# An FFN whose opening is ordered by the kernel's list scheduler, with paced loads, one more ordinary f-tile, and w2's two parts kept in DRAM

## The chip, the core and the metric

The kernel runs on one core of one Trainium2 chip. The metric is the device time of one execution in microseconds. TensorE is called PE, VectorE DVE, ScalarE ACT, GpSimd POOL and SyncE SP, as in the profile. PE multiplies, DVE, ACT and POOL work elementwise, and SP issues nearly all DMA transfers, in the order of its own instruction stream.

## The reference

One sequence of 2048 tokens with 640 channels goes through two layers, each with an adaptive layer norm in front and a gate behind. The first layer is a long convolution whose kernel is made from 128 complex exponentials per channel; the second is a gated FFN with 1728 hidden channels.

```python
mod = (_silu(c) @ w_mod).reshape(c.shape[0], 6, 1, -1)
sa, ca, ga, sb, cb, gb = (mod[:, 0], mod[:, 1], mod[:, 2], mod[:, 3], mod[:, 4], mod[:, 5])
h = _layernorm(x, axis=-1) * (1 + ca) + sa
x = x + ga * _A_ref(h, ...)          # rfft, product with the kernel's rfft, irfft, skip
h = _layernorm(x, axis=-1) * (1 + cb) + sb
gate, up = einsum("bsd,df->bsf", h, w1), einsum("bsd,df->bsf", h, w3)
x = x + gb * einsum("bsf,fd->bsd", _silu(gate) * up, w2)
```

Everything is in float32, and the FFN's products keep nearly that precision: each operand is split into a high part (rounded to the form that PE multiplies at full rate, `F32R`) and the remainder, and three products are summed: high by high, high by remainder, remainder by high (`three`, L839).

## The kernel before

**Two ways of ordering.** The first part of the kernel, the convolution, is a graph of tasks. `Plan.add` (L178) gives each task an engine, a duration, the tasks that it waits for, a rank and the buffers that it takes and gives back. `Plan.place` (L187) is a list scheduler: it always starts the task that can start first, and among those that can start within 0.1 us of each other the one of lowest rank. The ranks of most tasks are the long table `RANKS`; a task that is added with `own=True` keeps the rank in its `add`. `Plan.run` (L269) then issues all tasks in this order, and `InOrder` (L147) makes each engine keep it strictly. The second part, the FFN, is written as a program in `ffn` (L1002); there PE keeps the program's order, and the compiler places the instructions of the other engines.

**The convolution's end.** The channels go through the convolution in five blocks of 128. Its spectra end as `zd` in DRAM: each block stores eight pieces of 256 KB (`zt`, L1520 to L1530). The tokens' rows come back from them by one more product, the inverse: `iz` tiles are loaded from `zd`, multiplied by `wd` and added to the input `x2`. The FFN works on four token blocks of 512 tokens, so `x2[b]`, b = 0 to 3, each with four rows of 128 tokens by 640 channels. For blocks 0 and 1 the inverse of the first 512 channels (`cut`) is done before the FFN, in four units of two rows, u = 0 to 3 (`load_z` and `first_rows`, L1221 to L1230). The last 128 channels come from the fifth channel block, so their loads (`izb`, `last_rows`, L674) and products (`last_inverse`, L684) stand at the head of `ffn`. The task `change` (L1200) frees the memory of the kernel generation and issues the loads of `x2[0]` and `wd`; the tasks `fw` and `fs` load and split the weights of the f-tiles 0 and 13.

**The FFN.** The 1728 hidden channels are 13 f-tiles of 128 and a half one, number 13, with 64 gate and 64 up channels in one tile of 128. The token blocks go in two pairs, p = 0 with blocks 0 and 1, p = 1 with blocks 2 and 3. There are two ways to compute a tile's gate and up for both blocks of a pair. `plain` (L937) does one block with 30 matmuls of 128x512 (15 for tile 13). `group` (L883) does both blocks with 54 instead of 60: it multiplies sums and differences of weight halves (`factors`, L819) and of token blocks (`x_sums`, L750, which makes `T1` to `T4`), seven block products in place of eight. In pair 0 the tiles 0 and 13 are plain and 1 to 12 are groups; in pair 1 tile 13 is plain and 0 to 12 are groups.

The hidden tile times `w2` is `down` (L975): 15 matmuls (10 for tile 13) into five accumulators `acc`, one for each 128 output channels. The accumulators are five PSUM banks, so one block at a time: the even block's `down` runs inside the next group (`mid`, L1051), while the odd block's hidden tiles are kept in SBUF. After a pair's groups `late` (L1072) finishes the even block, writes it to the output (`output`, L985: gate on ACT, four PE transposes, an add on DVE; then `store`) and does all 14 `down` of the odd block, in the order 13, 0, 1 to 12. During the first `late` the blocks 2 and 3 are normalized, transposed (`turn_x`, L725) and split for pair 1. The second `late` ends the kernel. The inverse rows 8 to 15, for blocks 2 and 3, run inside the groups 1 to 8 of pair 0 (`inverse_row(7 + m)`, L1055).

**w2.** Each use of a tile of `w2` loads 320 KB (`down_load`, L782) and splits it (`down_split`, L793): the high part on ACT, the remainder on DVE or POOL. That is done for each of the four blocks. The high part, the remainder and the raw tile have two buffers each.

**The opening in order** (L1002 to L1034): the last inverse for blocks 0 and 1; block 0's norm, transposes and splits; `plain(0)` for tiles 0 and 13; the same preparation of block 1; `down` of tile 0; `plain(1)` for tile 0; `down` of tile 13; `plain(1)` for tile 13; the sums `T`; then group 1. POOL does every second remainder of the x splits, two of the four subtractions for `T`, and the weight sums.

Of the kernel before, what the change touches and what calls it, by code (L numbers as in the profile page):

```python
# [10 lines left out]
F32 = mybir.dt.float32  # L11
# [7 lines left out]
P = 128  # L19
L = 2048  # L20
D = 640
# [9 lines left out]
WA = 2  # L31
# [249 lines left out]
class K:  # L281
# [18 lines left out]
    def setup(self):  # L300
# [11 lines left out]
        self.zd = d.tile([32, 2, 64, D], F32, name="zd")  # L312
        self.xv = self.x.rearrange("(t1 q j) d -> q t1 j d", t1=32, q=4, j=NJ)
# [319 lines left out]
    def inverse_load(self, name, pool, tag, bufs, j0, nj, d0, d1, other=None):  # L633

        zv = self.zd.rearrange("f r t d -> (f r) t d")
        z = [pool.tile([P, nj, d1 - d0], F32, name=f"{name}{pr}", tag=f"{tag}{pr}", bufs=bufs) for pr in range(2)]
        for pr in range(2):
            for g in range(2):
                t0 = 16 * (2 * pr + g) + j0
                (other if g and other else self.nc.sync).dma_start(z[pr][g * 64:(g + 1) * 64], zv[:, t0:t0 + nj, d0:d1])  # L640
        return z

    def inverse(self, j0, nj, z, ps, tag, bufs, d0, d1):
        nc = self.nc
        w = d1 - d0
        for j in range(nj):
            for o, n in ((0, w),) if w <= 512 else ((0, 320), (320, 320)):
                py = ps.tile([P, 512], F32, name=f"iy{j0 + j}_{d0 + o}", tag=tag, bufs=bufs)
                for pr in range(2):
                    nc.tensor.matmul(py[pr * 64:(pr + 1) * 64, :n], self.wd[(j0 + j) // 4][:, (j0 + j) % 4, pr, :], z[pr][:, j, o:o + n],  # L650
                                     start=True, stop=True, tile_position=(0, pr * 64))
                x2 = self.x2[(j0 + j) // 4][:, (j0 + j) % 4, d0 + o:d0 + o + n]
                nc.vector.tensor_add(x2, py[:, :n], x2)

    def inverse_unit(self, u, pool, ps, tag, bufs):
        z = self.inverse_load(f"iz{u}", pool, "iz", 2, 2 * u, 2, 0, D)
        self.inverse(2 * u, 2, z, ps, tag, bufs, 0, D)


# [13 lines left out]

    def last_rows(self, b, cut):  # L674

        z = [self.row(f"izb{b}{pr}")[:, :512].rearrange("p (j d) -> p j d", j=4) for pr in range(2)]
        zv = self.zd.rearrange("f r t d -> (f r) t d")
        for pr in range(2):
            for g in range(2):
                t0 = 16 * (2 * pr + g) + 4 * b  # L680
                (self.nc.scalar if g else self.nc.sync).dma_start(z[pr][g * 64:(g + 1) * 64], zv[:, t0:t0 + 4, cut:])
        return z

    def last_inverse(self, b, z, cut):  # L684

        py = self.bank(f"iyb{b}").rearrange("p (j d) -> p j d", j=4)
        for j in range(4):
            for pr in range(2):
                self.pe.matmul(py[pr * 64:(pr + 1) * 64, j], self.wd[b][:, j, pr, :], z[pr][:, j], start=True, stop=True, tile_position=(0, pr * 64))
        x2 = self.x2[b][:, :, cut:]  # L690
        self.nc.vector.tensor_add(x2, py, x2)
# [22 lines left out]
    def ln_norm(self, b, rstd, nb):  # L714
        xn = []
        for j in range(4):
            x = self.row(f"xn{b}{j}")
            if j % 2:
                self.nc.vector.tensor_scalar(x, self.x2[b][:, j, :], rstd[:, j:j + 1], nb[:, j:j + 1], op0=ALU.mult, op1=ALU.add)
            else:  # L720
                self.nc.scalar.activation(x, self.x2[b][:, j, :], AF.Identity, scale=rstd[:, j:j + 1], bias=nb[:, j:j + 1])
            xn.append(x)
        return xn

    def turn_x(self, b, k, xn, X, v, where, pool):  # L725

# [1074 lines left out]
```

## Time and profile before

| | us |
|---|---|
| median of 3 runs | 1042.61 |
| lowest and highest | 1042.16, 1042.9 |
| the profiled execution | 1043.67 |
| its span in the profile | 1041.9 |
| PE busy | 883.4 (85%) |
| DVE busy | 734.5 (70%) |
| ACT busy | 576.8 (55%) |
| POOL busy | 410.2 (39%) |

The span runs from the first to the last instruction of the profile, and all positions below are counted from its start. A busy PE is not PE at its peak: matmuls are pipelined, one overlaps the next, and PE's clock is granted by a throttle (PEclk, 1.00 is full speed). So the start-to-start distance of a row of matmuls is the price of one, not its duration. "Idle before" is the time in which the engine did nothing just ahead of an instruction, and its releaser is the event that came last. In the chain of waits the last instruction is followed back, at each step to what released it; "issue" is time in which the engine waited for nothing that the profile shows. `SPq` and `ACTq` rows are the issuing of DMA transfers, and the time from issue to landing is that of the data.

### The profile page before, as it was taken

To read this page: it belongs to the slowest core of one execution; us is meant where nothing else is said; L and a number is where in the kernel's file an instruction comes from. 1 tells how busy PE (TensorE), PEld (TensorE's weight loads), DVE (VectorE), ACT (ScalarE), POOL (GpSimd) and SP (SyncE) were. 2 spreads that over 40 slices of the span, in tenths; PEclk is the share of its full clock that TensorE was granted. 3 is DMA by queue.
4 is the path that set the end of the run, shared out by engine and by line. 5 is a ranking of instruction groups with operands and counts; after the bars stand their busy time and mean duration, and the time that the engine had idled before them with its cause. 6 is when DMAs were issued, how large, how long until landed. Compare 5 with 4: busy or idle time off the path is not lost.

```text
span 1041.9 us, 20733 instructions
## 1 busy us (share of the span) xinstructions
PE 883.4 (85%) x7979; PEld 693.5 (67%) x7979; DVE 734.5 (70%) x1400; ACT 576.8 (55%) x1070; POOL 410.2 (39%) x423
## 2 busy tenths in 40 slices
PE   1474887798999873879999999997889999999897
PEld 1142756677788741756777788775668888888685
DVE  7998999999999375777767675566365656655422
ACT  6867888889788330543444454554254444444432
POOL 1798798888996010231111111134221121120141
PEclk9987999999999897888999999999999999999998
DMA  9965355423223889212333222341222212220332
GB/s 216 259 211 158 95 129 139 102 72 84 63 63 82 197 218 239 64 51 62 92 90 99 64 57 57 89 114 51 75 64 65 75 51 64 69 58 13 84 94 76
DMA packets 108540, 104.38 MB, mean 100 GB/s; under 512 B 10393, under 2 KB 90521, under 8 KB 107161
## 3 DMA queue, kind: packets, MB, share of 16 engines
q1 hardware_dynamic: 107352, 102.53, 36.6%
q8 instruction: 63, 1.03, 0.4%
q10 hardware_dynamic: 1088, 0.52, 0.2%
q14 instruction: 37, 0.30, 0.1%
HBM read 82.06 MB, written 20.97 MB: 99 GB/s over the span
## 4 chain that ended last, share of the span: by engine, by line
PE 64%; DVE 18%; DMA 8%; issue 4%; ACT 4%; SPq 1%; POOL 0%; POOLq 0%; DVEq 0%; ACTq 0%
PE c L156 18%; PE acc L156 17%; PE X L156 12%; PE ps L156 4%; DVE yy L156 3%; PE kps L156 2%; PE fk L156 2%; PE fz L156 2%; PE fh L156 2%; DVE xx L156 2%; DVE hn L156 2%; DVE fp L156 2%; DMA sp<-in_w_mod 2%; DMA xs<-in_x 2%; PE iy L156 1%
## 5 line engine op out<-in xcount | busy, mean ns | idle before, releaser
L156 PE MATMUL acc<-ah,w2l 128*128 128x512 f32 x280 | 115.4, 412 | 10.7 <-DVE w2l L662 6.4
L156 PE MATMUL acc<-ah,w2h 128*128 128x512 f32 x280 | 116.4, 416 | 9.1 <-ACT ah L661 4.4
L827 POOL TENSOR_TENSOR s<-wr 128x256 f32<-128x256 f32 x25 | 19.0, 762 | 225.2 <-DVE wl L662 96.5
L156 PE MATMUL acc<-al,w2h 128*128 128x512 f32 x260 | 105.2, 405 | 2.9 <-DVE al L662 2.9
L156 POOL TENSOR_TENSOR yy<-e,e 128x512 f32<-128x512 f32 x80 | 86.2, 1094 | 16.1 <-PE kps L156 11.2
L661 ACT ACTIVATE w2h<-w2r 128x640 fp32r<-128x640 f32 x51 | 37.5, 734 | 97.0 <-PE acc L156 81.4
L662 DVE TENSOR_TENSOR w2l<-w2r,w2h 128x640 fp32r<-128x640 f32 x37 | 34.6, 934 | 77.9 <-ACT w2h L661 77.9
L156 POOL TENSOR_TENSOR ph<-p,p 128x1024 int32<-128x1024 int32 x40 | 79.0, 1976 | 6.1 <-ACT tr L156 5.3
L156 PE MATMUL kps<-yy,xx 128*32 128x64 f32 x2560 | 51.3, 234 | 30.9 <-DVE xx L156 20.7
L661 ACT ACTIVATE wh<-wr 128x256 fp32r<-128x256 f32 x100 | 41.7, 418 | 62.6 <-PE X L156 46.9
L156 DVE TENSOR_TENSOR yy<-yy,tr 128x512 f32<-128x512 f32 (+1 forms) x80 | 75.4, 945 | 0.9 <-ACT tr L156 0.6
L156 PEld LDWEIGHTS acc<-ah,w2l 128*128 128x128 f32 x280 | 55.5, 198 | 25.7 <-DVE w2l L662 7.7
L156 PEld LDWEIGHTS kps<-yy,xx 128*32 128x32 f32 x2560 | 44.8, 116 | 40.8 <-issue 24.9
L156 PEld LDWEIGHTS acc<-ah,w2h 128*128 128x128 f32 x280 | 55.4, 198 | 24.1 <-ACT ah L661 5.5
L889 ACT ACTIVATE t<-g 128x512 f32<-128x512 f32 x50 | 31.6, 632 | 60.9 <-DVE g L853 60.9
L661 ACT ACTIVATE wh<-s 128x256 fp32r<-128x256 f32 x100 | 41.0, 410 | 43.2 <-PE c L156 20.6
L156 PEld LDWEIGHTS acc<-al,w2h 128*128 128x128 f32 x260 | 50.8, 195 | 15.3 <-DVE al L662 4.1
L662 DVE TENSOR_TENSOR wl<-s,wh 128x256 fp32r<-128x256 f32 x100 | 42.8, 429 | 23.1 <-ACT wh L661 21.0
L828 POOL TENSOR_TENSOR s<-s,wr 128x256 f32<-128x256 f32 x25 | 19.1, 763 | 98.0 <-issue 84.3
L858 DVE SCALAR_TENSOR_TENSOR g<-t,g 128x512 f32<-128x512 f32 x50 | 34.6, 693 | 32.4 <-ACT t L889 32.1
L662 DVE TENSOR_TENSOR wl<-wr,wh 128x256 fp32r<-128x256 f32 x100 | 43.8, 439 | 19.2 <-ACT wh L661 19.2
L156 ACT ACTIVATE tr<-ph,hpi 128x512 f32<-128x512 f32 x80 | 54.7, 691 | 3.6 <-DVE xx L156 2.0
(386 smaller groups left out, 2584.8 us busy)
## 6 DMA issues: line engine op xcount, KB each, us to landing
wr<-in_w SPq DMA_DIRECT2D x52, 320.0 KB, 3.8
w2r<-in_w SPq DMA_DIRECT2D x52, 320.0 KB, 2.9
zd<-zt SPq DMA_DIRECT2D x40, 256.0 KB, 2.8
xs<-in_x SPq DMA_DIRECT2D x16, 320.0 KB, 10.6
hs<-hb SPq DMA_DIRECT2D x20, 256.0 KB, 2.3
xb<-hs SPq DMA_DIRECT2D x20, 256.0 KB, 4.5
x<-in_x SPq DMA_DIRECT2D x16, 320.0 KB, 7.0
iz<-zd SPq DMA_DIRECT2D x32, 160.0 KB, 3.4
```

The costliest lines, as they stand in the source:

```text
L156: self.prev = self.k.order(f(*a, **kw), self.prev)
L661: self.nc.scalar.activation(H, v, AF.Copy)
L662: eng.tensor_tensor(Lo, v, H.bitcast(F32), op=ALU.subtract)
L827: G.tensor_tensor(s[0], u[:, 0:2], u[:, 2:4], op=ALU.add)
L828: G.tensor_tensor(s[1], s[0], g[:, 0:2], op=ALU.subtract)
L858: V.scalar_tensor_tensor(g, th, 1.0, g, op0=ALU.add, op1=ALU.mult)
L889: tanh = lambda o, i: A.activation(o, i, AF.Tanh, scale=0.5)
```

## The change

The change has four parts.

1. **The opening is a set of tasks.** `tail_tasks` replaces the tasks `fx`, `fw`, `fs`, `iz`, `ir` and the opening of `ffn` up to and without group 2. Each load, product, add, norm, transpose, split and gate of blocks 0 and 1 is a task of its own with its own rank; so the list scheduler orders it together with the convolution's end, and every engine keeps this order. Its `border` task opens the FFN's memory when the convolution's last stores and the rows 0 to 3 are done. POOL is left out of it: the remainders, the `T` subtractions and the sums run on DVE. The ten last ranks of `RANKS` go away.
2. **Loads.** They are issued in the order `x2[0]`, `wd[0]`, z units 0 and 1, weights and `w2` of tiles 0 and 13, `x2[1]`, `wd[1]`: 25 transfers. Each of the first 25 (`LOADS`) waits for the one two places before it (three places from the thirteenth on). Then come `izb0`, z unit 2, `izb1`, z unit 3. `wd[2]`, `wd[3]` and `x2[2]`, `x2[3]` are loaded after the opening.
3. **Tile 1 of pair 0 is plain.** Groups 2 to 12 follow. The inverse rows 8 to 15 move one group on (`inverse_row(6 + m)` in groups 2 to 9), and group 2 has no pending `down`, since that of tile 1 is done in the opening.
4. **w2's parts are made once.** In pair 0 a tile of `w2` is loaded and split as before, into one tile of two parts (`[P, 2, D]`, three buffers), and written to DRAM (`w2d`). Blocks 1, 2 and 3 load both parts, 640 KB, and split nothing.

With these, `late` is rewritten: all work that POOL had there goes to DVE; the odd block's hidden split and the reload of `w2` are issued one and two tiles ahead; the gate on ACT (`gated`) is apart from `output`, and the transposes and stores of the even block are spread over the loop of `down`. The order of the last block's end stays.

```diff
-        for k in range(KT):
-            self.output(2 * p, acc, k)
-        self.store(2 * p)
+        w2 = {i: self.w2_get(b, self.H[i]) for i in range(2)}
...
+        a = hidden(0)
         self.down(acc, *pend, True)
+        oc = [self.gated(2 * p, acc, k) for k in range(KT)]
+        acc = self.accumulators(b)
...
+        for k in range(KT):
+            at((k + 1) // 2, lambda k=k: self.output(2 * p, oc[k], k))
+        for q in range(4):
+            at(3 + 2 * q, self.store, 2 * p, 0, D, (q,))
...
+        for i, m in enumerate(self.H[:last]):
+            if i + 2 < n:
+                w2[i + 2] = self.w2_get(b, self.H[i + 2])
+            nxt = hidden(i + 1) if i + 1 < last else None
+            self.down(acc, m, a, w2.pop(i), i == 0, i == n - 1)
+            a = nxt
+            for f, args in extra.get(i, ()):
+                f(*args)
```
```diff
+    def w2_make(self, m, w2r):
+        t = self.w2_high(m, w2r)
+        self.w2_low(m, w2r, t)
+        self.w2_keep(m, t)
+        return t[:, 0], t[:, 1]
+
+    def w2_get(self, b, m):
+        t = self.w2_tile(f"w2{b}_{m}")
+        self.nc.sync.dma_start(t.bitcast(F32), self.w2d[m])
+        return t[:, 0], t[:, 1]
...
+    def paced(self, dst, src):
+
+        ins = self.nc.sync.dma_start(dst, src)
+        n = len(self.pace)
+        if 1 < n < LOADS:
+            self.tc.add_manual_dep(ins.ins, self.pace[-2 if n < 13 else -3].ins.name,
+                                   mybir.DependencyInfo(mybir.DependencyClass.Sync, mybir.DependencyReason.DATA), reason="pace")
+        self.pace.append(ins)
+
+    def tail_tasks(self, border, cut):
...
+        add("border", None, 0, border, ends + [f"ia{j}" for j in range(4)] + ["change"], 0)
...
+        add("izb0", "SP", 0, lambda: last_load(0), ends, -100, dma=[131072] * 4, take=[("w2", 1)])
+        load_z(2)
+        add("izb1", "SP", 0, lambda: last_load(1), ends + ["border", "izb0"], -99, dma=[131072] * 4)
+        load_z(3)
+        rows(1, 30)
...
+            add(f"iyb{b}", "PE", 1.9, lambda: last_inv(b), [f"izb{b}", f"lwd{b}", "border"] + (["tp0.4"] if b else []), 16.0, take=[("gu", 1)] if b == 0 else [])
+            add(f"iab{b}", "DVE", .7, lambda: last_plus(b), [f"iyb{b}"] + [f"lx{b}.{q}" for q in range(4)], rank, give=[("gu", "iyb0"), ("w2", "izb0")] if b == 0 else [])
...
+            add(f"ln{b}", "DVE", 3.9, lambda: ln_rest(b), [f"isb{b}"] + [f"is{j}.{c}" for j in range(4 * b, 4 * b + 4) for c in range(2)], rank)
...
+        prepare(0, 16)
+        prepare(1, 31)
...
+        plain(0, (0, 13), "pp0.", 17, [])
+        plain(1, (0, 13), "pp1.", 33, [])
+        load_up(1)
+        load_down(1)
+        used = [f"pp1.{x}" for x in (1, 3, 1, 3, 4)]
+        raw_split(1, 34, used)
+        down_split(1, 52)
+        plain(0, (1,), "pq0.", 35, ["pp1.4"])
+        plain(1, (1,), "pq1.", 36, ["pq0.4"])
...
+        pend = self.groups(0, range(2, 13), X, self.acc, W[2], (w2[2][:, 0], w2[2][:, 1]), None)
```

In `tail_tasks`, `tp`, `v`, `xh`, `xl` are the transpose, the shift, the high part and the remainder of one block of 128 channels; `iy`, `ia`, `is` the product, the add and the statistics of one inverse row; `xn` a normalized row; `gt`, `gs`, `gm`, `gh`, `gl` a hidden tile's gate and split; `dn` its `down`; `ws` and `wh2`, `wl2` the sums and splits of group 2's weights.

638 lines of the change are left out of this document (413 added, 225 removed), and 2 rows, old and new, of the table RANKS.

## The prediction

> **What bounds the kernel now.** I read the busy time by stretch first: seven stretches, cut where the PE's own rows change their work (columns: length; busy time and instruction count of PE, weight load, DVE, ACT, POOL; granted clock; DMA share; GB/s).
>
> ```profile
> 337.00:387.00 50.00, 42.28 (x578) 32.93 (x574) 28.07 (x62) 19.28 (x38) 3.46 (x5) 0.90 0.81 207
> 387.00:420.50 33.50, 13.83 (x69) 7.72 (x69) 18.83 (x79) 3.94 (x6) 0.31 (x1) 0.71 0.99 222
> 420.50:482.50 62.00, 50.36 (x200) 37.71 (x199) 44.63 (x64) 29.45 (x55) 19.40 (x16) 0.85 0.19 54
> 482.50:668.80 186.30, 186.30 (x815) 143.84 (x813) 127.33 (x283) 84.62 (x179) 31.08 (x41) 1.00 0.26 75
> 668.80:765.40 96.60, 78.32 (x332) 60.33 (x332) 54.60 (x69) 45.06 (x75) 30.36 (x22) 0.92 0.28 78
> 765.40:969.80 204.40, 204.40 (x892) 167.53 (x891) 121.30 (x223) 95.04 (x199) 33.29 (x45) 1.00 0.22 60
> 969.80:1041.90 72.10, 60.26 (x262) 47.55 (x260) 23.99 (x30) 25.01 (x39) 17.64 (x12) 0.94 0.32 87
> ```
>
> The two group loops (482 to 669 and 765 to 970) have PE busy all of the time at full clock: nothing but fewer matmuls shortens them. Time can be won only in the opening (337 to 482), in the first `late` (669 to 765) and in the second (970 to the end). Next, the chain of waits, for what ends last in the opening and for the pace of the loops (start, length, what):
>
> ```profile
> 344.04 4.55 issue
> ...
> 367.69 1.38 ACT wh_u L156 x5
> ...
> 387.22 7.91 DMA zd<-zt
> ...
> 395.14 9.16 DMA iz<-zd
> ...
> 404.44 1.19 PE iy L156 x5
> ...
> 407.07 1.55 DVE st L156 x8
> ```
> ```profile
> 487.27 3.43 PE acc L156 x15
> ...
> 504.87 3.44 PE acc L156 x15
> ...
> 670.87 5.30 PE acc L156 x15
> ...
> 801.18 3.43 PE acc L156 x15
> ...
> 816.97 3.43 PE acc L156 x15
> ```
>
> Fifteen matmuls in 3.43 us are 0.229 us each. A group takes 816.97 - 801.18 = 15.79 us, or 17.60 with an inverse row (504.87 - 487.27), so a row costs 1.81. Last, PE's timeline of the opening (start, length, form, count, idle before and its releaser):
>
> ```profile
> 415.90 4.91 PE L156 MATMUL tp<-ident,xn 128*128 128x128 f32 x20 [6.87 <-ACT xn L721]
> 420.47 0.78 PE L156 MATMUL gu<-x0h,wh_u 128*128 128x512 f32 x1
> ...
> 431.44 2.35 PE L156 MATMUL tp<-ident,xn 128*128 128x128 f32 x20
> ...
> 442.37 0.39 PE L156 MATMUL gu<-x4h,wh_u 128*128 128x512 f32 x1
> ...
> 482.30 0.39 PE L156 MATMUL X<-x0h,wh 128*128 128x512 f32 x1
> ```
>
> Block 0's first FFN matmul is at 420.47, block 1's at 442.37, group 2 starts at 482.30. Twenty transposes at full clock take 2.35.
>
> **The opening, part by part.** *Loads.* SP's queue issues them now in this order (start, length, what, count):
>
> ```profile
> 384.50 2.12 SPq L156 DMA_DIRECT2D x<-in_x  x4
> 386.71 1.03 SPq L156 DMA_DIRECT2D zd<-zt  x2
> 387.85 7.86 SPq L156 DMA_DIRECT2D iz<-zd  x8
> ```
>
> Four loads of 320 KB and eight of 256 KB stand around the last two `zd` stores; so the last store lands after 7.91 us and the z rows that read it after 9.16. After, at most two or three of the 25 early loads are in flight, `x2` of blocks 2 and 3 comes later, and `izb0` is issued first behind the stores. What such transfers take in calmer stretches (out<-in, KB each, median us to landing, over the whole span):
>
> ```profile
> wr<-in_w SPq DMA_DIRECT2D x52, 320.0 KB, 3.8
> w2r<-in_w SPq DMA_DIRECT2D x52, 320.0 KB, 2.9
> zd<-zt SPq DMA_DIRECT2D x40, 256.0 KB, 2.8
> ...
> iz<-zd SPq DMA_DIRECT2D x32, 160.0 KB, 3.4
> ```
>
> I take 3.5 for the store and 5 for `izb0`, with a paced load or two beside it: 17.1 becomes 8.5. *Stores issued earlier.* The 4.55 us in which PE waited for nothing the profile shows fall into a stretch of full DMA, and the tail's splits (the `wh_u` row) stand on the chain ahead of the convolution's last products. Finer tasks of later rank and calmer queues should give back some of it: between 0 and 10 us; I take 6, so the last store is issued at 381. *From landing to the first FFN matmul* there are 16.2 us now (404.3 to 420.5). The last two rows of block 1, which stand first there (404.4 to 408.6), move behind block 0, and so do block 1's add and stats, which interleave with block 0's norm: minus 4.2 and about 1, so 11. Block 0 starts at 381 + 3.5 + 5 + 11 = 400.5.
>
> *Block 0 to block 1* takes 21.9 us now, with PE work for 13. Block 1's own rows, stats, norm, transposes and splits now wait for `iz2`, `izb1`, `iz3` and run on DVE: I take 20, so 420.5. The extra plain tile fills what follows: block 1's 45 matmuls, 40 of `down` (tiles 0, 13, 1) and 60 for tile 1, in all 145 x 0.229 = 33.2; with 2.8 for a cold clock and a wait, group 2 starts at 456.5. It then has no pending `down` of tile 1 (-3.43) but one row more to go (+1.81). Gain of the opening: 482.3 - 456.5 + 3.43 - 1.81 = **27.4**. Against group 1 the plain tile costs 6 matmuls, 1.4 us, inside this count.
>
> *DVE as the cover.* DVE takes over POOL's share. These rows are of 387 to 483 (line, form, count | busy, mean ns | idle before):
>
> ```profile
> L662 DVE TENSOR_TENSOR x4l<-v,x4h 128x512 fp32r<-128x512 f32 x1 | 1.8, 1778 | 0.0
> ...
> L662 DVE TENSOR_TENSOR x5l<-v,x5h 128x512 fp32r<-128x512 f32 x1 | 0.7, 678 | 0.0
> ```
> ```profile
> L662 POOL TENSOR_TENSOR x5l<-v,x5h 128x512 fp32r<-128x512 f32 x1 | 1.7, 1737 | 0.0
> ```
>
> The same subtraction takes 0.68 on DVE alone, but 1.78 while POOL does its own of 1.74. From block 0's last add (389) to group 2, DVE has about 56 operations of 512 columns (38 us at 0.68), 24 bn_stats (5), two norm chains (8) and 17 weight splits and sums with two `w2` remainders (9): 60 in 67.5 us. It fits, barely; that is a rival.
>
> **The first `late`.** 332 PE instructions: 250 matmuls and 80 transposes (and two of the next group) need 250 x 0.229 + 4 x 2.35 = 66.7 us; it takes 96.6. PE's groups there say why:
>
> ```profile
> L156 PE MATMUL acc<-ah,w2h 128*128 128x512 f32 x75 | 33.2, 442 | 4.7 <-ACT ah L661 2.0 <-DVE ah L880 1.6 <-ACT w2h L661 0.8
> L156 PE MATMUL acc<-ah,w2l 128*128 128x512 f32 x75 | 33.2, 442 | 9.6 <-DVE w2l L662 6.4 <-POOL w2l L662 3.2
> ...
> L156 PE MATMUL to<-ident,oc 128*128 128x128 f32 x40 | 6.6, 312 | 4.0 <-ACT oc L989 3.1 <-DVE x L994 0.6 <-DVE h L965 0.4
> ```
>
> Of the 18 us of waits, 10.4 are for `w2` parts, 3.1 for `oc`, 1.6 for tile 13's `ah`; the rest of the 30 is clock, as in the 5.30 us for 15 matmuls at 670.87 after a wait. After, `w2` arrives split: its ACT and DVE or POOL steps fall away, and a reload of 640 KB takes their place. It is issued two tiles ahead, when `down` of the tile before last frees its buffer, so it has 2 x 3.43 = 6.9 us. No row shows a transfer of 640 KB; between 2.9 (as 320 KB) and twice that, 5.8, I take 4.5: hidden. `oc` is computed before the matmuls that cover it. What stays: the 2.0 us for tile 12's `ah`, its cold 1.9, and DVE, which alone now has 52 operations of 512 or 640 columns (13 hidden remainders, 5 outputs, 2 norms, 6 shifts, 10 x remainders, 16 for `T`) and 12 of 256 (0.43): 40 us, against 54 of PE in the loop. For that I leave 9 us of waits and cold clock; the bounds are 0 and what it loses now. 66.7 + 3.9 + 9 = 79.6: gain **17**.
>
> By a rule of the Trainium skill (TensorE: Matmul & The Clock Gate, Part 1), the clock halves only after an idle window of about 3.4 us, and the ramp stays under 1% of a span. Here 2.04 us were enough, and the ramps of this `late` alone are about 12 us; by the rule the sum would be some 4 us lower, since the waits that stay would cost no ramp.
>
> **The second `late`.** 220 matmuls and 40 transposes need 50.4 + 4.7 = 55.1; with 6 us from the last matmul's end to the last store, 11 are lost of 72.1: the wait for `ah` of tile 12, the wait at tile 13, the ramps. The output's transposes move into the loop and tile 13 is split ahead: gain **4.6**, between 0 and 7. The loop ran without gaps already, so here the reload can only cost.
>
> **Covered at nothing:** `w2`'s writes to DRAM in pair 0 (640 KB in a group of 17 us, at a DMA share of 0.26) and the wider loads in pair 1 (0.22). Uncovered, a group would wait for SP, some 1 us each.
>
> Sum: 27.4 + 17 + 4.6 = 49. The profiled execution took 1043.67 (span 1041.9), 1.06 above the median of 1042.61. 1043.67 - 49 = 994.7, against the median 993.6: I say **994**.
>
> **Rivals.** *DVE becomes the bound of the opening.* For: 60 us of work, every step a ping-pong with ACT, and DVE was busy only 44.63 of 62 us there. At that 0.72, 60 us take 83: group 2 at 472, gain 12 instead of 27: 1009. Against: POOL's contention is gone. *The `late` loops are bound by reloads and DVE.* 640 KB and a quarter of a 1.3 MB store in 3.43 us are 239 GB/s, and the full queues of 387 to 420 moved 222. Then the second gains nothing and the first 6: 33, so 1009. Both: 18, so 1025.
>
> *Slower: pacing starves the tail.* SP issues in order; a paced load that waits holds back the `zd` stores and all reloads behind it. The crowded landings of 335 to 490:
>
> ```profile
> x<-in_x SPq DMA_DIRECT2D x16, 320.0 KB, 7.0
> iz<-zd SPq DMA_DIRECT2D x16, 256.0 KB, 8.2
> ```
>
> If loads still take 8 us with two in flight, the 25 take 100 and end at 437, not at 385 (3.8 each, two at a time). The last store behind them puts block 0 at 437 + 19.5 = 456.5 and group 2 at 512.5: the opening loses 28.6, the whole 7: 1050. It decides from a landing of 7.4 us on, 3.7 between loads, where the opening's loss eats the 21.6 of the two `late`. Against: an uncrowded 320 KB lands in 2.9 to 3.8. The Trainium skill (DMA: Bandwidth & Descriptors, Rules for kernel authors) wants 1 MiB and more per DMA for full bandwidth, which speaks against two of 320 KB in flight. By its fit of 2.0 us plus bytes at 436 GB/s, an estimate of 2.75 us a load, 25 would still end near 366.
>
> *The order doesn't hold:* the opening's fixed order waits for early mistakes of its durations and its gain is nil: 1021.
>
> **How the numbers follow.** Forecast 0.57; DVE-bound opening 0.16, `late` bound 0.11, both of them or no gain in the opening 0.07, pacing 0.09. With the best ends of the unknown costs (last store at 377, blocks 16 apart, no cold clock, the first `late` at its 70.6, the second 7) it is 38 + 26 + 7 = 71, with the worst (store at 387, `late` 12, second 0) 33; hardly all at once, so the forecast's own range is 980 to 1010. For 8 in 10 it reaches up to the rivals: 980 to 1021. A measurement of this kernel tells about 0.2%, 2 us, from no change. Faster 0.9, the same 0.01, slower 0.09.
>
> **What would show it.** Right: `izb0` lands within 9 us of the last store's issue, block 0's first FFN matmul near 400, group 2 near 456, no wait for `w2l` in either `late`. Wrong: DVE full with PE waiting on `T` or `x` remainders up to group 2; `acc` waiting for a DMA of `w2`; paced loads landing past 390; either group loop below full PE.

## The result and the profile after

The changed kernel takes 993.97 us (median of 4 runs, 988.81 to 995.51) against 1042.61 (4 runs): a ratio of 0.9525 with an interval of 0.949 to 0.956. The forecast was 994, the range 980 to 1021. A later repetition gave 992.82 (5 runs) and 0.9512 [0.9496, 0.9528]. The profiled execution took 993.93, its span 992.1, 49.8 less than before.

The busy time by stretch, cut where PE's work changes (columns as in the prediction):

```profile
337.00:377.70 40.70, 39.54 (x606) 30.70 (x604) 27.83 (x58) 20.03 (x40) 0.63 (x1) 1.00 0.68 179
377.70:408.30 30.60, 11.98 (x68) 8.29 (x68) 17.81 (x52) 8.21 (x12) 0.00 (x0) 0.67 0.99 245
408.30:460.40 52.10, 48.51 (x212) 39.57 (x211) 40.33 (x95) 26.28 (x47) 3.31 (x4) 0.97 0.64 187
460.40:646.10 185.70, 185.70 (x809) 141.45 (x807) 126.63 (x288) 82.66 (x176) 26.94 (x36) 1.00 0.36 108
646.10:720.00 73.90, 68.60 (x332) 56.50 (x331) 43.86 (x70) 36.44 (x61) 3.86 (x4) 0.98 0.55 169
720.00:925.50 205.50, 205.50 (x894) 167.34 (x892) 111.04 (x211) 85.35 (x186) 32.61 (x44) 1.00 0.27 81
925.50:992.10 66.60, 57.74 (x261) 46.12 (x260) 18.96 (x29) 16.77 (x26) 0.00 (x0) 0.95 0.51 158
```

Three stretches became shorter. Group 2 starts 21.9 us earlier, the first `late` is 22.5 shorter and the second 5.4; of the two loops, still full of PE work, the first is 0.7 shorter and the second 0.6 longer. In sum 49.8 (each rounded).

The chain of waits through the opening (start, length, what):

```profile
345.85 0.42 issue
...
376.57 4.17 DMA zd<-zt
...
381.60 8.25 DMA izb<-zd
```

The stall of 4.55 us in which PE waited for nothing visible is down to 0.42, and the last `zd` store (it follows its `issue` row) is issued 10.6 us earlier (376.57 for 387.22). But the row load behind it, `izb`, takes 8.25 us, hardly less than the 9.16 of before: the stretch around it has the DMA engines busy 0.99 of the time. It has four parts of 128 KB; the first two landed after 2.9 and 3.4 us, the last after 8.25. PE's timeline then shows what stands before the first FFN product of block 0 (start, length, form, count, idle before and its releaser):

```profile
397.56 4.85 PE L156 MATMUL tp<-ident,xn 128*128 128x128 f32 x20 [5.64 <-DVE xn L156]
403.80 1.16 PE L156 MATMUL iyb<-x6hizb,wd 128*64 128x128 f32 x16 [1.39 <-ACT v L156]
...
407.80 0.59 PE L156 MATMUL iy<-x3liz,wd 128*64 128x512 f32 x1
408.32 0.50 PE L156 MATMUL gu<-x0h,wh_u 128*128 128x512 f32 x1
...
426.34 0.48 PE L156 MATMUL gu<-x4h,wh_u 128*128 128x512 f32 x1
...
460.41 0.39 PE L156 MATMUL X<-x0h,wh 128*128 128x512 f32 x1
```

Between block 0's transposes (`tp`) and its first product (`gu`) PE waits 1.39 us until ACT has read the transposes' last bank, and then does block 1's whole inverse, its last columns (`iyb`) and its rows (`iy`, 16 products), for 4.5 us.

In the first `late`, two waits of PE are left, 5.1 us in all (count | busy, mean ns | idle before, releaser), and the page gives the landing of the reload:

```profile
L156 PE MATMUL acc<-ah,w 128*128 128x512 f32 x150 | 46.7, 397 | 2.0 <-ACT ah L635 2.0
L156 PE MATMUL to<-ident,oc 128*128 128x128 f32 x40 | 6.8, 332 | 3.1 <-ACT oc L971 3.1
```
```profile
w<-w2d SPq DMA_DIRECT2D x42, 640.0 KB, 3.9
```

The second `late` keeps three small waits (us in total, times, longest):

```profile
PE acc L156 <- ACT ah L635: 2.0, 1, 2.0
PE acc L156 <- DMA w<-w2d: 1.0, 1, 1.0
PE to L156 <- ACT oc L971: 0.3, 1, 0.3
```

### The profile page after: what moved, and what is told of

The parts are those of the page before. It is cut to its first block, busy times and chain, and to the rows that moved or that the text cites. A ratio compares the mean times of both kernels' runs of the same rounds, so it can differ in the third digit from the quotient of the medians.

```text
span 992.1 us, 20566 instructions
## 1 busy us (share of the span) xinstructions
PE 864.0 (87%) x7985; PEld 684.6 (69%) x7985; DVE 700.1 (71%) x1393; ACT 547.9 (55%) x1024; POOL 341.1 (34%) x371
## 4 chain that ended last, share of the span: by engine, by line
PE 68%; DVE 13%; DMA 8%; ACT 5%; issue 3%; SPq 1%; ACTq 0%; DVEq 0%
PE c L156 18%; PE acc L156 18%; PE X L156 12%; PE gu L156 3%; PE ps L156 3%; DVE yy L156 3%; PE fk L156 3%; PE kps L156 2%; PE fz L156 2%; PE fh L156 2%; DMA sp<-in_w_mod 2%; DVE xx L156 2%; DVE hn L156 2%; DVE fp L156 2%; PE iy L156 1%
## 5 line engine op out<-in xcount | busy, mean ns | idle before, releaser
L156 PE MATMUL acc<-ah,w 128*128 128x512 f32 x560 | 174.1, 397 | 5.1 <-ACT ah L635 4.1
L156 PEld LDWEIGHTS acc<-ah,w 128*128 128x128 f32 x560 | 104.5, 189 | 28.7 <-ACT ah L635 6.7
L156 PE MATMUL acc<-al,w 128*128 128x512 f32 x260 | 102.7, 395 | 0.1
L636 DVE TENSOR_TENSOR wl<-s,wh 128x256 fp32r<-128x256 f32 x92 | 38.8, 423 | 67.9 <-ACT wh L635 67.5
L812 POOL TENSOR_TENSOR s<-wr 128x256 f32<-128x256 f32 x22 | 16.3, 741 | 190.3 <-DVE wl L636 116.3
L813 POOL TENSOR_TENSOR s<-s,wr 128x256 f32<-128x256 f32 x22 | 16.7, 758 | 137.5 <-issue 137.4
L814 POOL TENSOR_TENSOR s<-wr 128x256 f32<-128x256 f32 x22 | 17.0, 774 | 129.3 <-DVE wl L156 98.2
L156 PEld LDWEIGHTS acc<-al,w 128*128 128x128 f32 x260 | 49.2, 189 | 12.3 <-DVE al L636 1.3
L842 DVE SCALAR_TENSOR_TENSOR g<-t,g 128x512 f32<-128x512 f32 x48 | 33.7, 701 | 31.6 <-ACT t L873 31.3
L156 DVE TENSOR_TENSOR xx<-tr,xx 128x512 f32<-128x512 f32 x80 | 54.5, 683 | 0.7 <-ACT tr L156 0.7
L156 ACT ACTIVATE tr<-ph 128x512 f32<-128x512 int32 x80 | 47.4, 599 | 13.0 <-DVE yy L156 7.2
L156 PE MATMUL ps<-wk,ks 128*64 128x128 f32 x640 | 42.0, 283 | 13.5 <-DVE ks L156 8.9
L156 PE MATMUL ps<-wk,xb 128*64 128x128 f32 x640 | 47.2, 301 | 6.5 <-ACT sp L156 3.3
```

The costliest lines, as they stand in the source:

```text
L156: self.prev = self.k.order(f(*a, **kw), self.prev)
L636: eng.tensor_tensor(Lo, v, H.bitcast(F32), op=ALU.subtract)
L812: eng.tensor_tensor(s[0], u[:, 0:2], u[:, 2:4], op=ALU.add)
L813: eng.tensor_tensor(s[1], s[0], g[:, 0:2], op=ALU.subtract)
L814: eng.tensor_tensor(s[2], g[:, 0:2], u[:, 0:2], op=ALU.subtract)
L842: V.scalar_tensor_tensor(g, th, 1.0, g, op0=ALU.add, op1=ALU.mult)
```

## The experiments

The stages of every kernel, from PE's timelines: where group 2 starts, the first loop, the first `late`, the second loop, the second `late` up to the end of the span. All are taken from the profiled execution, the median and the ratio from all runs: 2 of e6, e7 and e9, 4 to 10 of the others. "Ratio" is to the kernel before, on the same chip.

| kernel | group 2 | loop 1 | late 1 | loop 2 | late 2 | span | median | ratio, interval |
|---|---|---|---|---|---|---|---|---|
| before | 482.3 | 186.4 | 96.3 | 204.9 | 72.0 | 1041.9 | 1042.6 | |
| changed | 460.4 | 185.7 | 73.9 | 205.6 | 66.6 | 992.1 | 994.0 | 0.9525 [0.949, 0.956] |
| changed, again (e13) | 458.9 | 185.7 | 74.9 | 205.6 | 65.8 | 990.9 | 992.8 | 0.9512 [0.950, 0.953] |
| e1 no pacing | 465.6 | 185.7 | 73.8 | 205.6 | 67.2 | 997.8 | 1000.0 | 0.9593 [0.955, 0.964] |
| e2 split again | 465.9 | 185.7 | 73.8 | 205.6 | 65.4 | 996.4 | 994.5 | 0.9535 [0.948, 0.959] |
| e3 early gate | 459.5 | 185.7 | 73.9 | 205.7 | 67.4 | 992.2 | 993.6 | 0.9525 [0.948, 0.957] |
| e4 x2 later | 455.4 | 185.6 | 73.8 | 205.2 | 66.8 | 986.7 | 990.9 | 0.9504 [0.946, 0.955] |
| e5 plain tile alone | 473.1 | 191.5 | 94.1 | 205.1 | 72.0 | 1035.8 | 1037.7 | 0.9948 [0.993, 0.997] |
| e6 reload alone | 482.5 | 186.4 | 121.9 | 204.3 | 81.3 | 1076.3 | 1079.4 | 1.0357 [1.026, 1.046] |
| e7 one load in flight | 492.0 | 185.7 | 74.7 | 205.6 | 65.8 | 1023.8 | 1027.6 | 0.9861 [0.976, 0.996] |
| e9 POOL's splits to DVE | 482.6 | 186.4 | 85.7 | 205.1 | 66.9 | 1026.7 | 1027.9 | 0.9863 [0.977, 0.995] |
| e10 reload, both buffers | 482.9 | 186.4 | 88.5 | 204.3 | 80.8 | 1042.8 | 1045.4 | 1.0017 [1.000, 1.004] |
| e11 two buffers | 459.1 | 185.7 | 82.0 | 205.6 | 79.3 | 1011.7 | 1013.7 | 0.9722 [0.970, 0.974] |
| e12 combined | 457.3 | 185.6 | 70.6 | 209.1 | 65.3 | 987.8 | 988.5 | 0.9474 [0.946, 0.949] |

Where group 2 starts differs between executions even where the code up to it is alike: from 458.9 to 465.9 in the five kernels changed, e13, e2, e3 and e11. Most of that lies in the convolution: e2 changes nothing there, and yet it reaches the point of the stall (345.85 in the changed kernel) only at 349.45. So the start of group 2 alone is not read to better than some 7 us, and distances from a point shortly before are compared instead; the stages behind it repeat within about 1.

### The loads: pacing, one in flight, x2 later

**e1** takes the pacing out.

```diff
-        if 1 < n < LOADS:
-            self.tc.add_manual_dep(ins.ins, self.pace[-2 if n < 13 else -3].ins.name, ...)
```

> The changed kernel with the waits between the paced loads taken out; every engine keeps the same order of instructions. If pacing is what makes the opening's transfers land soon, the flood is back: PE's stop of some 4.5 us for nothing the profile shows returns near 345, the convolution's end and the last zd stores move 3 to 5 us later, block 0's first FFN matmul goes from 408.3 to 411 to 417, and the time is 997 to 1003. If the order alone brings the gain, all stays within 1 us of 994. If pacing only holds loads back, block 0 starts 3 to 5 us earlier and the time is 989 to 991.

It takes 1000.0 us, against 994.5 and 993.6 for e2 and e3 on the same chip, which keep the pacing; the intervals of the ratios overlap, so the distances within the profile decide. Its chain has the stall of the kernel before again, at the same point of the convolution:

```profile
345.46 4.09 issue
...
380.61 4.01 DMA zd<-zt
```

The six kernels without pacing all have it (4.09 to 4.55 us; e5, e6, e9 and e10 keep the opening of the kernel before), and none with pacing has more than 0.6. From that point to the issue of the last store there are 43.2 us in the kernel before (344.04 to 387.22), 35.2 without pacing (345.46 to 380.61) and 30.7 in the changed kernel (345.85 to 376.57); the six other paced kernels that keep this chain have 30.5 to 31.0. So pacing is worth 4.4 of these 12.5 us, 3.7 of them the stall itself, and the rest of the new opening 8.0.

PE's rows don't show what it waits for in the stall, but the trace's DMA packets point at something. In all 13 kernels that have this row of PE (e7 has not), a transfer of 16 KB on the queue that the profile calls `instruction` (q8) ends 1.35 to 1.73 us before PE goes on. In the six kernels with the stall it starts 13.7 to 14.5 us after the one before it on that queue, and only once PE already stands (1.4 to 2.1 us into the stall); in the seven others it starts 9.4 to 9.9 us after, and before PE gets there. So PE most likely waited for its next instructions, whose transfer came late among the many loads. No run tried that by itself.

**e7** goes the other way, to one load in flight.

```diff
-        if 1 < n < LOADS:
-            self.tc.add_manual_dep(ins.ins, self.pace[-2 if n < 13 else -3].ins.name,
+        if 0 < n < LOADS:
+            self.tc.add_manual_dep(ins.ins, self.pace[-1].ins.name,
```

> The changed kernel with the paced loads held to one in flight: each waits for the landing of the one before instead of the second or third before. Theory of the prediction's pacing rival (the loads then come too late for the work that needs them): block 0's first up product 15 to 35 us after 408.3, total 1008 to 1030. Rival (the stream has slack, since two in flight already filled the queues; the inverse's rows then land faster): block 0 within 5 us of 408, total 989 to 1000. Either way, if fewer loads in flight speed up the row load of block 0, it lands in less than the 8.25 us it took.

Block 0 starts at 439.9, 31.6 us later, so the first theory holds; the chain is now mostly the loads themselves, one behind the other:

```profile
378.93 3.73 DMA iz<-zd
382.72 3.21 DMA wr<-in_w
385.94 3.10 DMA wr<-in_w
```

Up to 402, a load of 256 or 320 KB that has the queues nearly to itself lands in 3.1 to 3.9 us here. Block 0's row load, last issued at 404.0, has landed by 408.7, as the expectation's last sentence allowed. This is the pacing rival of the prediction brought about on purpose. It costs 34 us and still leaves the kernel 1.4% below the one before.

**e4** issues `x2[1]` and `wd[1]` behind `izb0`, unpaced.

```diff
-LOADS = 25
+LOADS = 20
...
         load_down(13)
-        load_x2(1)
-        load_wd(1)
...
         add("izb0", "SP", 0, lambda: last_load(0), ends, -100, dma=[131072] * 4, take=[("w2", 1)])
+        load_x2(1)
+        load_wd(1)
         load_z(2)
```

> The changed kernel with block 1's x2 and wd loads issued behind izb0 and izb1, not ahead of and between them. If izb0's 8.25 us come from sharing the queues with them, it lands in 4 to 5 us, block 0's first FFN matmul moves from 408.3 to about 404.5, group 2 from 460.4 to about 457, and the time is 990 to 991. If block 1 then waits for the later x2 or the later z units, block 0 gains the 3 to 4 us and block 1 loses them: the time stays within 1 us of 994.

```profile
379.94 4.54 DMA izb<-zd
...
398.43 1.16 PE iyb L156 x16
399.59 1.72 PE iy L156 x8
401.31 0.90 PE gu L156 x3
```

The row load lands in 4.54 us where it took 8.25, and only half of block 1's row products stand before `gu`. Block 0 starts 28.4 us behind the convolution's last product instead of 33.9; block 1 gives 2 of it back. The median is 3 us below that of the changed kernel, but the intervals overlap: the time alone doesn't prove it. The landing does: it took 4.61 in e12, which has the same two loads moved, and 7.75 to 8.62 in the six kernels that issue them first.

### The plain tile alone

**e5** is the kernel before with tile 1 of pair 0 made plain.

```diff
-        sums, part, W = self.factors(0, 1, raw)
+        one = self.whole(1, raw)
...
+        h1, = self.plain(0, X, [(1, one)])
         for i in range(2):
             self.x_sums(X, [v[0, i], v[1, i], v[0, 2 + i], v[1, 2 + i]], 0, i, "tmp", 7)
+        self.plain(1, X, [(1, one)])
...
+        self.down(acc, 1, h1, w21, False, False)
...
-        pend = self.groups(0, range(1, 13), X, acc, W, w2, None)
+        pend = self.groups(0, range(2, 13), X, acc, W, w2, None)
```

> The kernel before, with one thing of the change alone: f-tile 1 of blocks 0 and 1 is done in the ordinary way (its two up products, gate and down products for each block), the differences T1 to T4 are made between its two halves, and the groups begin at f-tile 2; loads, splits by POOL and the late stage stay as they were. Theory (the extra ordinary tile gives TensorE about 25 us of matmuls while VectorE makes the differences, which stood before group 1 in the kernel before; group 1 held TensorE 27.3 us for some 16 us of its own period): group 2 starts 8 to 12 us earlier than 482.3, total 1031 to 1035. Rival (VectorE and ScalarE bound this stretch, so the order of TensorE's work does not matter): group 2 starts less than 3 us earlier, total 1040 or more.

Group 2 does start 9.2 us earlier, but the total gains only about 5 us, since 5.1 come back in the loop. PE's timeline of group 2:

```profile
478.48 0.80 PE L156 MATMUL c<-x1h,wh 128*128 128x512 f32 x1 [3.89 <-DVE h L959]
479.07 0.63 PE L156 MATMUL c<-x1l,wh 128*128 128x512 f32 x1
479.49 0.63 PE L156 MATMUL c<-x1h,wl 128*128 128x512 f32 x1
```

PE ran ahead of DVE: it waits 3.89 us for the gate of block 1's tile, and the matmuls behind the wait come 0.43 apart instead of 0.23. The start of group 2 came as the theory had it, the total did not. The tile covers the `T` work, and then the next thing that DVE owes is late. In the changed kernel, where the scheduler orders DVE as well, no such wait is left.

### w2: the reload, the order, POOL

**e2** is the changed kernel, but blocks 1 to 3 load `w2` and split it again, as before; only the order and the buffers are the new ones.

```diff
     def w2_get(self, b, m):
-        t = self.w2_tile(f"w2{b}_{m}")
-        self.nc.sync.dma_start(t.bitcast(F32), self.w2d[m])
+        w2r = self.w2_load(m)
+        t = self.w2_high(m, w2r)
+        self.w2_low(m, w2r, t)
         return t[:, 0], t[:, 1]
```

> The changed kernel, but the blocks 1, 2 and 3 load the raw w2 tile and split it again on ACT and DVE, in the new order two tiles ahead. If the w2 parts were what the first late waited for, it goes from 73.9 us back up by 8 to 15 with waits for w2l, the second late by 1 to 3, and the time is 1002 to 1010. If the new order (splits ahead, transposes and stores spread) brings the gain by itself, the first late stays below 77, and the time is 994 to 998.

The first `late` of e2, in the same columns:

```profile
651.60:725.40 73.80, 68.55 (x331) 56.47 (x331) 54.80 (x85) 45.65 (x76) 4.49 (x5) 0.98 0.37 103
```

It lasts 73.80 as against 73.90, with 11 us more of DVE and 9 of ACT, and with the same two waits of PE (2.0 and 3.1 us); the second `late` is 1.2 shorter, as no load is waited for. The reload is worth nothing here.

**e6** is the opposite: the kernel before, with the reload and its old order.

```diff
+            w = [self.wp.tile([P, D], F32R, name=f"w2{x}{b}_{m}", tag=f"w2{x}", bufs=2) for x in "hl"]
+            for i in range(2):
+                dma(w[i].bitcast(F32), self.w2d[m, i])
+            return w
```

> The kernel before, with the other part of the change alone: the two parts of w2 are kept in DRAM when they are first made, and blocks 1 to 3 reload both parts (two loads of 320 KB) in place of the load and split; the order of the late stages, one tile ahead and two buffers each, stays. Theory of the prediction (the waits for w2's parts in the first late stage vanish because w2 comes back split already): the stage between the two runs of groups takes 84 to 90 us instead of 96.3, total 1030 to 1036. Rival (the waits went with the new order, two tiles ahead in three buffers; a reload of twice the bytes one tile ahead only puts a transfer where the split was): that stage takes 93 us or more, total 1038 or more.

The reload makes that stage 25.6 us longer. One tile of its loop, from SP's queue and PE's timeline, and PE's waits for the high parts in the whole stage:

```profile
719.58 0.32 SPq L793 DMA_DIRECT2D w2l<-w2d  x1
719.99 0.38 SPq L793 DMA_DIRECT2D w2h<-w2d  x1
```
```profile
716.10 0.47 PE L156 MATMUL acc<-ah,w2h 128*128 128x512 f32 x1 [2.69 <-DMA w2h<-w2d]
...
719.39 0.40 PE L156 MATMUL acc<-al,w2h 128*128 128x512 f32 x1
...
723.43 0.76 PE L156 MATMUL acc<-ah,w2h 128*128 128x512 f32 x1 [3.65 <-DMA w2h<-w2d]
```
```profile
PE acc L156 <- DMA w2h<-w2d: 28.2, 9, 4.4
```

The load is issued when the products of the tile at hand end (719.39) and the next tile waits for it: nothing covers it. The reason is partly the experiment's own. Block 2's part of tile 13 was loaded at the fifth tile and held one of the two buffers until the stage's end.

**e10** moves that one load behind the stage.

```diff
-                w13 = self.down_load(2, 13)
...
-        w13 = self.down_split(2, 13, w13)
+        w13 = self.down_load(2, 13)
```

> As the kernel before with w2's parts reloaded, but block 2's part of f-tile 13, which the run before this loaded early and which held one of the two buffers through most of the first late stage, is loaded after that stage. Theory (with both buffers in use each load has one tile's down products, 3.4 us, to hide behind, against 3.6 us from its issue to the data): the first late stage falls from 121.9 to 84 to 92 us and the second stays at 80 or so, whose loads wait behind the stores of block 2; total 1040 to 1052, so still not below the kernel before by more than 3 us. Rival (the prediction's reason: the waits of the kernel before vanish once w2 comes back split): the first late stage 75 to 84 us, total 1020 to 1034.

```profile
PE acc L156 <- DMA w2h<-w2d: 4.9, 3, 4.4
```

With two buffers the first `late` gains 7.9 us on the kernel before, and the second loses 8.8, as the loads there stand behind the stores of block 2 (four stores from 974.69 in SP's queue, the loads from 978.14) and PE waits 9.7 us for them in all. In all the reload in the old order is worth nothing (1.0017).

**e9** is the kernel before, with POOL's remainders of `w2` and of the hidden tiles in both `late` given to DVE. POOL keeps its other work, 14.5 of 30.4 us in the first `late`.

```diff
-                w2[i] = self.down_split(b, self.H[i], w2r.pop(i), nc.gpsimd if i % 2 else nc.vector)
+                w2[i] = self.down_split(b, self.H[i], w2r.pop(i), nc.vector)
...
-            a = self.hidden_split(b, m, self.h.pop(m), nc.gpsimd if i % 2 == 0 else nc.vector)
+            a = self.hidden_split(b, m, self.h.pop(m), nc.vector)
```

> The kernel before, with the remainders of w2 and of the hidden tiles in the first late stage all made by VectorE instead of by VectorE and POOL in turn; the order and the buffers stay. Theory A (what TensorE waited for there were POOL's slow splits and the contention between POOL and VectorE): the stage takes 80 to 88 us instead of 96.3, total 1026 to 1034. Theory B (it waited because each tile's split starts only one tile ahead, in two buffers, behind the rest of the queue): 93 us or more, total 1038 or more.

These two lines are worth 14 us (by the interval 5 to 24, from two runs); the stages show where: 10.7 us in the first `late`, as theory A had it, and 5.0 in the second. PE's waits for `w2` parts there fall from 10.4 to 5.5 us. The remainder `w2l` in the first `late`, in the kernel before and then in e9 (form, count | busy, mean ns):

```profile
L662 DVE TENSOR_TENSOR w2l<-w2r,w2h 128x640 fp32r<-128x640 f32 x7 | 7.5, 1074 | 14.8 <-ACT w2h L661 14.8
L662 POOL TENSOR_TENSOR w2l<-w2r,w2h 128x640 fp32r<-128x640 f32 x7 | 10.9, 1556 | 36.0 <-ACT w2h L661 29.2 <-PE tp L156 6.8
```
```profile
L662 DVE TENSOR_TENSOR w2l<-w2r,w2h 128x640 fp32r<-128x640 f32 x14 | 11.5, 822 | 14.5 <-ACT w2h L661 14.3
```

POOL takes 1556 ns for what DVE does in 822 when POOL has none of these remainders, and in 1074 when it has half of them. The Trainium skill (GPSIMD Engine Reference, 1. Specifications) says that the two share their memory interfaces, with contention when a DVE instruction has two inputs from there; these rows agree. DVE carries twice as many of them and is busy only 1.7 us longer (56.25 for 54.60).

**e11** is the changed kernel with each reload of the late stages held until the tile two before it is done.

```diff
-            if i + 2 < n:
-                w2[i + 2] = self.w2_get(b, self.H[i + 2])
             nxt = hidden(i + 1) if i + 1 < last else None
-            self.down(acc, m, a, w2.pop(i), i == 0, i == n - 1)
+            end = self.down(acc, m, a, w2.pop(i), i == 0, i == n - 1)
+            if i + 2 < n:
+                w2[i + 2] = self.w2_get(b, self.H[i + 2], end)
```

> The changed kernel with each reload of the late stages held until the down products of the tile two before it are done, as if there were two buffers instead of three. Theory (it is the third buffer, not the reload, that takes the waits away): each late stage grows by 3 to 10 us with waits for w2's loads at its head, total 999 to 1013. Rival (two buffers would do, since a tile's products are about as long as a load): each grows by less than 2 us, total 992 to 998.

The stages grow by 8.2 and 12.7 us, the second by more than the theory gave, and the total lies just above its range. In SP's queue four stores of `out` go ahead of two loads, and PE then stands:

```profile
665.58 3.30 SPq L987 DMA_DIRECT2D out<-x  x3
668.99 1.08 SPq L784 DMA_DIRECT2D w<-w2d  x1
671.93 0.34 SPq L784 DMA_DIRECT2D w<-w2d  x1
```
```profile
676.50 0.47 PE L156 MATMUL acc<-ah,w 128*128 128x512 f32 x1 [3.73 <-DMA w<-w2d]
```

The changed kernel has its four stores at the same place, from 665.33 on, with the loads behind them from 668.98, and doesn't wait there. So the lead that the third buffer gives is what lets the reload cost nothing. (A held load also holds back what stands behind it in SP's queue; that share was not separated.)

### The gated outputs, and a combined kernel

**e3** computes block 1's gated outputs `oc` before the plain products of blocks 2 and 3, since ACT idles there for 9.9 us.

```diff
+        oc = [self.gated(1, acc, k) for k in range(KT)]
         a, = self.plain(2, X, [(13, box["half"])])
         self.plain(3, X, [(13, box["half"])])
-        oc = [self.gated(1, acc, k) for k in range(KT)]
```

> The changed kernel with block 1's gates on ACT written ahead of the half tile's matmuls of blocks 2 and 3. ACT is idle there for 9.9 us, and PE then waits 3.1 us for oc. If that wait is only the order of ACT's queue, it goes, with 0 to 1.7 us of cold clock behind it: the first late takes 69 to 71 us and the time is 989 to 991. If the gates now hold up the half tile's tanh and its banks, a wait of 2 to 3 us comes back on the transposes or on the next group, and the time stays within 1 us of 994.

```profile
PE to L156 <- DVE x L980: 1.6, 1, 1.6
PE to L156 <- ACT aa L947: 0.9, 1, 0.9
```

The wait of 3.1 us for `oc` is gone, and two waits for banks stand in its place: 0.9 us for one that a plain tile's gate still reads, 1.6 for one that DVE's add of an earlier output still reads. Nothing is gained, the second of the two cases expected.

**e12** puts e4 and e2 together and moves the whole output of block 1 ahead of the plain products.

```diff
-        a, = self.plain(2, X, [(13, box["half"])])
-        self.plain(3, X, [(13, box["half"])])
         oc = [self.gated(1, acc, k) for k in range(KT)]
+        for k in range(KT):
+            self.output(1, oc[k], k)
+        a, = self.plain(2, X, [(13, box["half"])])
+        self.plain(3, X, [(13, box["half"])])
...
-        for k in range(KT):
-            self.output(1, oc[k], k)
```

> The changed kernel with three things put together: x2's and wd's later loads behind block 0's row load, w2 loaded and split again in blocks 1 to 3 instead of reloaded from DRAM, and block 1's gated outputs turned back before the ordinary up products of blocks 2 and 3 instead of behind them. Theory (the 3.1 us wait for the gated outputs is closed because ScalarE idles there for 9.9 us, the row load is 3 us faster, the last stage loses its wait for a load): the first late stage 70 to 71.5 us, the last 65.5, span 984 to 987.5, ratio to before 0.944 to 0.949. Rival (as when only the gates were moved, the waits move to the gates of the ordinary tiles): the first late stage 73 to 75 us, ratio 0.948 to 0.952.

```profile
642.86:713.44 70.58, 68.53 (x331) 56.34 (x331) 50.99 (x80) 43.14 (x72) 1.36 (x2) 0.98 0.44 119
713.44:922.54 209.10, 206.87 (x893) 168.35 (x891) 125.84 (x229) 97.43 (x204) 36.21 (x48) 0.99 0.20 55
```
```profile
719.27 0.47 PE L156 MATMUL c<-x2hT,wh 128*128 128x512 f32 x1 [2.23 <-DVE h L950]
```

The first `late` falls to 70.6, as expected, but the second loop grows by 3.5: its first group waits 2.23 us for DVE to gate tile 13 of block 3, which the outputs had covered. So this part nets about 1 us, and what is left is mostly the gain of the two others. It is still the fastest kernel, 988.5 against 992.8 for the changed one on the same chip, with intervals that don't meet.

**e13** is the changed kernel once more.

> The changed kernel once more, to stand beside the combined one on the same chip: 989 to 996, ratio to before 0.949 to 0.956. If the combined kernel is worth what its parts were, it is 4 to 8 us faster than this one.

It came out at 992.8, and e12 is 4.3 us faster.

## Why the prediction was right, and where its reasons were not

The opening, by the prediction's steps (us):

| step | predicted | measured |
|---|---|---|
| last store issued | 381 | 376.6 |
| it lands after | 3.5 | 4.2 |
| `izb0` landed after that | 5 | 9.1 |
| from there to block 0's first product | 11 | 18.5 |
| block 0 | 400.5 | 408.3 |
| to block 1 | 20 | 18.0 |
| to group 2 | 36 | 34.1 |
| group 2 | 456.5 | 460.4 |

Of the signs that it named, `izb0` within 9 us of the last store's issue failed (13.3); block 0 and group 2 came 8 and 4 us late, and by the spread of group 2 above only the distances in the table are firm.

**The store.** "Between 0 and 10 us; I take 6" was too little: 10.6. Of its two reasons, calmer queues are shown by e1, for 4.4 us; finer tasks were not tried alone. Its guess that the stall belongs to the full queues held: it goes with the pacing.

**The row load** was given 5 us "with a paced load or two beside it". It shared the queues with `x2[1]`, `izb1` and z unit 2; the last paced load, `wd[1]`, was issued at 391.17, so landings past 390, which the prediction named as a sign against it, did come. With `x2[1]` and `wd[1]` behind it (e4) it takes 4.54.

**Landing to first product.** Here a step failed. "The last two rows of block 1 ... move behind block 0 ... minus 4.2" did not happen, and the ranks say why. Block 0's products have rank 17, block 1's last columns (`iyb1`) 16.0 and its rows 16.7; of the tasks that can start within 0.1 us of each other, the scheduler takes the lowest.

```diff
+                add(f"iy{j}", "PE", .54, inv, ... 16.7 if b else rank, ...)
```

The transposes ended at 402.4, and the first remainder that the products need was done at 401.3, so they could have begun there. Instead came 1.39 us of waiting and 4.5 of block 1's inverse: 5.9 of the 7.5 us that were missed. The wait is one that the plan doesn't know: `iyb1` writes the bank of the last transposes, but is added behind these (`tp0.4`), not behind ACT's reading of them. Part of the 5.9 comes back, as block 1 follows 18.0 us later instead of 20. No run changed these ranks alone.

**Block 1 and the plain tile** were right within 2 us each, and so PE, not DVE, is the bound from block 0 on: 48.5 busy of 52.1. DVE was busy 53.5 us of the 68.4 from block 0's last add to group 2, where the prediction counted 60. That rival falls for the changed kernel, though e5 shows how near it is.

**The first `late`** was to take 79.6 and took 73.9. Over the 66.7 for the products, 12.9 had been set aside for waits and cold clock and 7.2 were used; two waits of 5.1 in all are left of 18.1, so 13.0 of the 22.5 are waits and the rest mostly the clock behind them (0.98 granted for 0.92). The 17 were right in sign, but a reason was wrong: "`w2` arrives split: its ACT and DVE or POOL steps fall away". e2 keeps these steps and is as fast; e6 and e10 drop them and gain 8 at most. What the waits of 10.4 us for `w2` parts came from was POOL, which was slow itself and slowed DVE (e9: 10.7 of the 22.5), and splits that start too late even without POOL (5.5 us of waits in e9). The rest, 11.8, goes with the new order and with the rest of POOL's work, which were not taken apart; that a lead of two tiles matters is shown by e11 for reloads alone. "`oc` is computed before the matmuls that cover it" is true of block 0, but the wait of 3.1 us was never block 0's: in the kernel before it stands at 761.05, at block 1's outputs, whose place the change keeps, and there it stayed (716.03).

**The second `late`** was to gain 4.6 and gained 5.4. e9 gains 5.0 there with no more than POOL's splits moved, so these can account for nearly all of it; the output's new place was not tried alone. `acc` did wait once for a load of `w2`, 1.0 us, a sign that the prediction had named against itself.

**The loops** were taken to gain the bookkeeping of 1.6 us and gained 0.0 in sum. The second is 0.6 longer, with the reload and without it (e2), so it isn't the reload; the cause was not tried.

The sum was near because the errors offset each other: the opening's 27.4 was 22.6 with the loop behind it, the two `late` made 27.9 instead of 21.6. That the median met the forecast to a tenth of a microsecond is luck.

Two sums of the rivals don't come out as written, without bearing on the forecast. 640 KB and a quarter of the store in 3.43 us are some 286 GB/s; 239 takes an eighth. And the ends of the loads at 437 and 385 count two in flight throughout, where from the thirteenth on there were three. Loads with the queues nearly to themselves took 3.1 to 3.6 us for 320 KB in e7, not the estimate's 2.75.

## What to carry to other kernels

When two changes are made at once, a wait that vanishes is not proof of the one named after it: do each alone, as the reload that seemed to clear these waits is worth nothing in either order and cost 37 us where it lost a buffer. An elementwise engine that is slower than its neighbour and disturbs it can cost more on the critical path than it takes off; two lines that gave half its work there away won 14 us by themselves. A list scheduler does what its ranks and its listed waits say, not what one remembers of them, so look up both for what stands directly ahead of the first product that everything waits for.

## What the runs showed of the hardware

- PE stalled for 4.09 to 4.55 us with no visible reason where many loads were in flight, at the same point of the program in six kernels, and for under 0.6 in the eight where at most three were. In the six, a 16 KB transfer of the `instruction` queue came some 4 to 5 us later behind the one before it than in the others, and PE went on 1.35 to 1.73 us after its end.
- A wait's length did not settle what the clock does next. In e6 the 15 matmuls behind a wait of 2.69 us took 3.5 us from 716.10, and those behind 3.65 took 6.0 from 723.43; waits of 3.65 to 3.75 halved the rate each of the five times there. The wait of 2.04 to 2.05 us for tile 12's `ah` stands in both `late` of every kernel: in the kernel before it was followed by half the rate at 670.87 and by the full rate at 972.15, in the changed one by the full rate at 648.30 and by half at 927.74. So the prediction read too much from one case when it took 2 us to be enough. The Trainium skill (TensorE: Matmul & The Clock Gate, Part 1) counts activity in a free-running window of some 3.4 us. That fits in that the same wait can go either way; that the clock halves only after such a window of idleness does not fit the waits of 2.04.
- A 640 KB load landed in 3.9 us (median of 42); loads of 320 KB took 2.9 (`w2r`) and 3.8 (`wr`) in the kernel before. Twice the bytes cost 1 us or less here.
